# A new matmul order, load order and scheduler model, and the head outermost in the q and k casts

## The chip, the cores and the metric

The kernel runs on one core of one Trainium2 chip. The metric is the device time of one execution in microseconds (us); most executions of one kernel agree within a few tenths of a per cent. Times were taken in several sessions, in each of which the kernel before ran beside the others on the same chip. Its own median moved from 226.7 to 227.4 us between sessions, so kernels are compared by their ratio to it in the same rounds. All results were correct.

## The reference

Sliding-window attention with four sink positions (batch 4, 8 heads, 768 positions, head size 64), then a feed-forward part on its 3072 x 512 output. Cut to what matters:

```python
scores = np.matmul(q, k.transpose(0, 1, 3, 2)) / np.sqrt(64)
keep = is_sink | in_window                 # 4 sinks, window of 128
a = softmax(np.where(keep, scores, -1e9))
x = (a @ v) as 3072 x 512
h = x @ w_in                               # 512 x 2048
g = h * (1.0 / (1.0 + np.exp(-beta * h)))
return g @ w_out                           # 2048 x 512
```

## The kernel before

The program builds a list of operations, and a scheduler written in the kernel file orders it when the program is built. The order of the matmul groups on the TensorE (PE) and of the first loads is fixed by two strings that a search found. One letter is one group: T transposes q and k, C and D are scores, S sink scores, A attention output, X its transpose, h and g the two halves of a first feed-forward product for an early tile (H when whole), O four matmuls of the second product, b a small transpose of beta.

```python
PAR = {'MD': 1, 'XB': 2, 'l0': [0, 2, 6, 1, 3, 4, 9, 5, 7, 10, 8],
       'mix': 'aawwaawawawwawwaaaawwawwawwwawaa'}   # a: a q, k or v load, w: a weight load
ORDER = ('TCDTSTTDCSDSCASCTADACbXXAhhhXXThghDghgDhggThgggChhgghgShDSghSghghTghgCASCAXADOXOAhhhhXOXOgOOggOOhghg'
...                                                  # 405 groups in all
class Graph:
    LEAD, PAD, LATE = 1500, 2000, 90000
    BIAS, EARLY = 300, 100000        # a copy on the activation engine counts 300 ns more
    FILL_TO = 48000                  # fillers may stand up to here (ns of the plan)
```

The scheduler estimates when each load lands and when each engine is free; each engine is then given its own list in that order, with semaphores to wait on. Where the plan sees PE idle before 48 us, it puts in a *filler*, a matmul of ones into a free PSUM bank that nobody reads, meant to keep the clock up:

```python
    def fillers(self, t, banks, holder, new):
        while self.free["pe"] < min(t, self.FILL_TO):
            ...
            n = min(512, int((t - now) * 2.4 / slow) // 128 * 128)
            if not free or n < 128:
                return
            ...                              # append one matmul of n columns
```

Weights are loaded as f32 in 16 pieces of 512 KB and cast to bf16 before use, and so are q, k and v:

```python
    def cast_w(j):
        ...
        any_of(copies(dst, src_, {"act": 947, "dve": 602, "gp": 1060}), ...)   # the engine is chosen by the plan
    def cast(hb, n, i):
        ...
            src = stg[n][z][:, hs, :, :].rearrange("p h j d -> p j h d")       # q and k of the first half batches
            dst = x16[n][hb % NX][:, :, hs, :]
```

The first product (line 910 before, 956 after) needs such weights: four h groups need the first, third, fifth and seventh weight load in turn, four g groups the second, fourth, sixth and eighth. The activation engine then takes a tanh of it and the vector engine (DVE) multiplies; both read PSUM, and the program lets a bank be written again only after both. In the profile of before, PE's operand loads (PEld) of line 783, which reads no product, waited 1.8 us for line 917's products, in five waits.

The softmax here doesn't subtract the row's maximum and nothing guards it: scores larger than these inputs give would overflow.

## Time and profile before

| | before |
|---|---|
| time, median of the first 3 runs | 226.73 us |
| span of the profiled run | 225.4 us |
| PE busy from 20 to 200 us | 177.1 of 180 us |
| fillers | 31, of which 29 before 20 us |
| first matmul of line 910 | 19.90 us |

PE is the engine to look at: from 20 us on it is nearly always busy, so the end is set by when its stream starts, by the stream's work and by the waits within it. The prediction shows the lines of the profile on which this rests.

### The profile page before, as it was taken

Reading aid. Unit: us, or ns where it says so; the run is one execution under the profiler, and the core shown is the slowest. Engines: PE = TensorE matmul, PEld = TensorE weight load, DVE = VectorE, ACT = ScalarE, POOL = GpSimd, SP = SyncE. Lnnn points to the kernel's source line nnn. Section 1 sums busy time; section 2 is a strip of 40 time slices with the busy share of each in tenths; the row PEclk is TensorE's granted clock in tenths of the full one; section 3 lists DMA queues with packets and bytes.
Section 4 is the critical chain, followed back from the end, with each engine's and each line's share of the span. In section 5 each row is a group of like instructions: output and inputs, shape, how many; then the busy total and the mean of one; then the engine's idle time right before and its main releaser. Section 6 shows DMA issues by size and latency. Waiting matters only on the chain.

```text
span 225.4 us, 4463 instructions
## 1 busy us (share of the span) xinstructions
PE 216.1 (96%) x1699; PEld 119.9 (53%) x1720; DVE 141.0 (63%) x313; ACT 141.6 (63%) x257; POOL 66.4 (29%) x157
## 2 busy tenths in 40 slices
PE   8789999999999999999999999999999999999994
PEld 3446555555455545645564665455455556555443
DVE  1798899878757278839774478756362626455100
ACT  2495998134882857547788847777756756566221
POOL 7174345000362616352108510141435400000000
PEclk9979999999999999999999999999999999999999
DMA  7999999998999989999999999993133033101112
GB/s 159 266 320 374 360 213 311 348 250 161 219 207 224 202 198 235 189 253 221 197 239 208 185 239 220 245 256 106 47 84 81 0 84 81 49 4 47 47 47 93
DMA packets 104741, 40.95 MB, mean 182 GB/s; under 512 B 93312, under 2 KB 97680, under 8 KB 104720
## 3 DMA queue, kind: packets, MB, share of 16 engines
q1 hardware_dynamic: 103152, 40.65, 79.4%
q8 instruction: 13, 0.21, 0.4%
q10 hardware_dynamic: 1568, 0.02, 0.4%
q14 instruction: 8, 0.07, 0.1%
HBM read 27.30 MB, written 6.29 MB: 149 GB/s over the span
## 4 chain that ended last, share of the span: by engine, by line
PE 70%; DVE 10%; SPq 8%; DMA 6%; ACT 3%; issue 1%
PE P L931 31%; PE P L910 28%; SPq L635 7%; DMA v_stage<-in_v_dram 5%; DVE g L917 4%; PE P L861 4%; PE P L783 3%; DMA out_dram<-osb 2%; PE P L851 2%; SPq L891 1%; ACT t L915 1%; PE P L819 1%; PE P L1027 1%; DVE onorm L868 1%; DVE vaug L563 1%
## 5 line engine op out<-in xcount | busy, mean ns | idle before, releaser
L910 PE MATMUL P<-xT,w_in 128*128 128x384 bf16 x512 | 92.7, 327 | 0.0
L915 ACT ACTIVATE t<-P,hbeta 128x384 f32<-128x384 f32 x128 | 71.8, 586 | 32.3 <-PE P L910 24.4
L931 PE MATMUL P<-w_out,g 128*128 128x512 bf16 (+2 forms) x379 | 89.1, 371 | 1.7 <-DVE g L917 0.4
L917 DVE SCALAR_TENSOR_TENSOR g<-t,P 128x384 bf16<-128x384 f32 x128 | 67.8, 548 | 34.5 <-ACT t L915 31.8
L798 POOL TENSOR_SCALAR_AFFINE_SELECT E<-E 128x256 bf16<-128x256 bf16 (+1 forms) x109 | 52.4, 512 | 57.7 <-ACT E L792 57.7
L910 PEld LDWEIGHTS P<-xT,w_in 128*128 128x128 bf16 x512 | 48.3, 98 | 34.8 <-issue 0.8
L931 PEld LDWEIGHTS P<-w_out,g 128*128 128x128 bf16 x400 | 36.6, 98 | 37.5 <-DVE g L917 1.5
L792 ACT ACTIVATE E<-P 128x768 bf16<-128x768 f32 (+1 forms) x64 | 45.6, 760 | 14.8 <-PE P L783 14.7
L861 PE MATMUL P<-vaug,E 128*128 128x65 bf16 x352 | 19.1, 197 | 0.3 <-DVE vaug L563 0.2
L861 PEld LDWEIGHTS P<-vaug,E 128*128 128x128 bf16 x352 | 17.1, 100 | 3.6 <-ACT E L792 0.7
L558 ACT ACTIVATE osb<-P 128x512 f32<-128x512 f32 (+2 forms) x16 | 9.1, 570 | 15.2 <-PE P L931 15.1
L868 DVE TENSOR_TENSOR onorm<-P,rden 128x384 bf16<-128x384 f32 x32 | 17.4, 552 | 0.5
L783 PE MATMUL P<-qkT 64*128 64x128 bf16 (+1 forms) x256 | 16.6, 241 | 1.0 <-ACT E L792 0.4
L823 ACT ACTIVATE ES<-P 128x128 bf16<-128x128 f32 (+1 forms) x32 | 12.0, 390 | 7.0 <-PE P L819 7.0
L563 DVE CAST k<-k_stage 128x512 bf16<-128x512 f32 (+1 forms) x24 | 11.5, 477 | 6.0 <-DMA k_stage<-in_k_dram 5.7
L783 PEld LDWEIGHTS P<-qkT 64*128 64x128 bf16 x256 | 8.2, 94 | 12.4 <-issue 3.9
L851 PE MATMUL P<-vS,ES 128*128 128x130 bf16 x64 | 12.9, 223 | 0.6 <-DVE vS L686 0.4
L563 DVE CAST q<-q_stage 128x512 bf16<-128x512 f32 (+1 forms) x19 | 8.8, 465 | 7.2 <-DMA q_stage<-in_q_dram 7.1
L563 DVE CAST vaug<-v_stage 128x512 bf16<-128x512 f32 x18 | 7.9, 439 | 8.2 <-DMA v_stage<-in_v_dram 8.0
L725 POOL TENSOR_TENSOR kS<-qkT,headm 128x8 bf16<-128x8 bf16 x16 | 3.0, 209 | 32.5 <-DMA qkT<-k 28.8
L1027 PE MATMUL P<-ones 128*128 128x512 bf16 (+2 forms) x31 | 9.8, 443 | 1.2 <-POOL ones L569 1.1
L564 DVE TENSOR_SCALAR osb<-P 128x512 f32<-128x512 f32 x9 | 6.2, 690 | 6.9 <-DMA out_dram<-osb 5.2
(48 smaller groups left out, 90.5 us busy)
## 6 DMA issues: line engine op xcount, KB each, us to landing
v_stage<-in_v_dram SPq DMA_DIRECT2D x24, 256.0 KB, 4.9
out_dram<-osb SPq DMA_DIRECT2D x23, 256.0 KB, 2.5
q_stage<-in_q_dram SPq DMA_DIRECT2D x18, 256.0 KB, 4.7
k_stage<-in_k_dram SPq DMA_DIRECT2D x18, 256.0 KB, 5.6
wst<-in_moe_w_in_dram SPq DMA_DIRECT2D x5, 512.0 KB, 6.7
wst<-in_moe_w_out_dram SPq DMA_DIRECT2D x4, 512.0 KB, 8.4
g<-in_moe_w_out_dram SPq DMA_DIRECT2D x4, 512.0 KB, 8.0
q_stage<-in_q_dram SPq DMA_DIRECT2D x8, 192.0 KB, 4.7
```

Source lines behind the costliest of these rows:

```text
L563: return lambda e: e.tensor_copy(dst, at())
L635: o = add("sp", lambda e: e.dma_start(dst, src), ns, w=[("stg", n, z, j) for j in keys], dma=f"d{n}{z}{'' if i is None else i}", ring={610 ...
L783: add("pe", lambda e, dst=dst, own=own, kc=kc, rows=rows, q0=q0, nq=nq: e.matmul(dst(), tokens(own, hp, 1, rows, kc, 1)[:, 0, :], tokens(h ...
L792: add("act", lambda e, src=src, dst_=dst_: e.activation(dst_, src(), AF.Exp, bias=0.0, scale=SCALE), act_ns(256 * n), w=[(k_, z, j) for k_ ...
L798: alts = {"gp": (lambda e, d=d, sg=sg, at_=at_: e.affine_select(d, d, [[0, 2 * len(at_)], [sg, 128]], ALU.is_ge, 0.0, base=min(sg, 0), cha ...
L851: add("pe", lambda e, m=m, o0=o0: e.matmul(A()[:, o0:o0 + 2 * (D + 1)], ES[z][:, (c0 + m) * 128:(c0 + m + 1) * 128], vS[b % 2][:, 2 * hp:2 ...
L861: e.matmul(A()[:, o0:o0 + D + 1], E[z][:, i, hh, :], vaug[vz][:, kb % NK, 2 * hp + hh, :], start=a, stop=o, skip_group_check=True), 39,
L868: add("dve", lambda e: e.tensor_tensor(onorm[:, on, 2 * c0:2 * c1, :], av()[:, :, 0:D], rden[on][:, 0:2 * nb].unsqueeze(2).to_broadcast([1 ...
L910: first = add("pe", lambda e, c=c: e.matmul(hp(), w_in16[:, c, m * 128:(m + 1) * 128], xT[:, hb, c, 128 * c0:128 * c1], start=(c == 0), st ...
L915: add("act", lambda e: e.activation(tt[ti][:, 0:n], hp(), AF.Tanh, bias=0.0, scale=hbeta[:, m:m + 1]), act_ns(n) + 93, r=["hbeta"], w=[("t ...
L917: add("dve", lambda e: e.scalar_tensor_tensor(gt[hb % NG][:, m, 128 * c0:128 * c1], tt[ti][:, 0:n], 1.0, hp(), ALU.add, ALU.mult), dve_ns( ...
L931: add("pe", lambda e, m=m: e.matmul(P[:, bk[0], a:b], gt[hb % NG][:, m, t * 128:(t + 1) * 128], w_out16[:, m, a:b], start=(m == 0), stop=( ...
```

## The change

The intent: the scheduler's model was to come closer to the chip (longer and more detailed transfer times, stalls, fillers that leave room for the cost of a change between kinds of matmul; its constants are its author's estimates, not checked one by one here), the search for the matmul order and the load order was done again against several cases of it (longer transfers, a lower clock; the search itself is not shown here), and the casts of q and k for the first half batches got another order of loops. The core of the diff, with cuts:

```diff
-PAR = {..., 'l0': [0, 2, 6, 1, 3, 4, 9, 5, 7, 10, 8], 'mix': 'aawwaawawawwawwaaaawwawwawwwawaa'}
-ORDER = ('TCDTSTTDCSDSCASCTADACbXXAhhhXXThghDghgDhggThgggChhgghgShDSghSghghTghgCASCAXADOXOAhhhhXOXOgOOggOOhghg'
+PAR = {..., 'l0': [0, 1, 3, 9, 2, 10, 5, 4, 7, 6, 8], 'mix': 'aaaawawawawwwwaaaawwwwwwawwaaaa'}
+ORDER = ('TSbCTDDSCTSDTCAADTSCXXTCSAhhAXhhXgggghhhhggghghDhggDhgTghShhDgCCThgSggSDAAACXOXOAOXhOXOhhOhghOOgggOh'
 ...
-    LEAD, PAD, LATE = 1500, 2000, 90000
-    BIAS, EARLY = 300, 100000
+    LEAD, PAD, LATE = 2000, 1000, 90000
+    BIAS, EARLY = 150, 16000
-    RING, FETCH, SWITCH = 165, 900, 85
-    DEPTH = 9
+    FETCH, SHORT, SWITCH = 1150, 400, 85
+    DMA = {"nat": ((434, 580, 580, 580, 470), 64, 1200, 115, 2250, 1200), ...   # one row per kind of transfer
+    DEPTH = 5
 ...                                    # place(), stall() and fillers() follow the new model
-            src = stg[n][z][:, hs, :, :].rearrange("p h j d -> p j h d")
-            dst = x16[n][hb % NX][:, :, hs, :]
+            src = stg[n][z][:, hs, :, :]
+            dst = x16[n][hb % NX][:, :, hs, :].rearrange("p j h d -> p h j d")
```

## The prediction

> **What bounds the kernel now.** I read the page's busy shares and its row of slices first, then the busy time of each engine in five stretches, then the timeline at the places where PE stood still. The stretches:
>
> ```profile
> 0.00:20.00 20.00, 16.58 (x151) 9.29 (x152) 13.50 (x34) 11.67 (x21) 12.21 (x40) 0.91 1.01 267
> 20.00:60.00 40.00, 39.18 (x306) 21.89 (x306) 34.64 (x73) 25.96 (x48) 9.22 (x20) 1.00 1.02 275
> 60.00:120.00 60.00, 58.53 (x503) 32.16 (x508) 41.35 (x97) 40.97 (x77) 23.03 (x51) 1.00 1.11 217
> 120.00:200.00 80.00, 79.37 (x618) 44.65 (x627) 44.88 (x99) 53.06 (x96) 21.92 (x48) 1.00 0.62 128
> 200.00:225.40 25.40, 22.40 (x129) 11.96 (x129) 6.64 (x12) 9.94 (x18) 0.00 (x0) 1.00 0.14 53
> ```
>
> After the length stand PE, weight loads, DVE, ACT and POOL, then granted clock, DMA share, GB/s. PE is the bound: from 20 us to 200 us it is idle for 0.82 + 1.47 + 0.63 = 2.92 us. The first 20 us are different: 3.4 us idle, and of the 16.58 us busy most is filler that computes nothing (the same stretches for line 1027):
>
> ```profile
> 0.00:20.00 20.00, 8.95 (x29) 0.91 1.01 267
> 20.00:60.00 40.00, 0.83 (x3) 1.00 1.02 275
> ```
>
> In that start the clock also fell once (windows of 1 us, same columns as the first table):
>
> ```profile
> 13.00:14.00 1.00, 0.51 (x10) 0.23 (x6) 0.95 (x4) 1.00 (x3) 1.00 (x3) 1.00 1.08 300
> 14.00:15.00 1.00, 0.98 (x14) 0.63 (x14) 1.00 (x4) 0.82 (x3) 1.00 (x3) 0.76 0.94 333
> 15.00:16.00 1.00, 1.00 (x16) 1.00 (x14) 1.00 (x5) 1.00 (x2) 0.29 (x2) 0.50 1.03 374
> 16.00:17.00 1.00, 1.00 (x9) 0.41 (x7) 1.00 (x2) 0.99 (x3) 0.81 (x1) 0.50 1.03 338
> 17.00:18.00 1.00, 1.00 (x17) 0.83 (x14) 0.89 (x5) 0.30 (x2) 0.80 (x2) 0.53 1.05 366
> ```
>
> PE was half idle just before (0.54 and 0.51 us in the two windows from 12 to 14), and then ran some 3.4 us at 0.50. The first matmul of the feed-forward part (line 910) starts at 19.90 us. From then on PE is nearly full, so the time of the end is about the start of that stream, plus its work, plus its waits.
>
> What limits the stream up to 60 us is the arrival of data: the DMA share is 1.02 and DVE is busy 34.64 of 40 us. The timeline shows two places. The eighth weight load, the last one of line 910's weights, lands at 29.54 us by the trace's semaphores, DVE casts it only at 30.55, and the matmul that needs it follows 0.1 us after the cast:
>
> ```profile
> 30.55 0.69 DVE L563 CAST w_in<-wst 128x1024 bf16<-128x1024 f32 x1
> ...
> 31.34 0.33 PE L910 MATMUL P<-xT,w_in 128*128 128x384 bf16 x1
> ```
>
> The second weight matrix does the same to line 931's first matmuls: the load lands at 37.17, the cast runs from 37.71 for 0.78 us, and PE, which had put in a filler, starts at 38.43.
>
> The later waits are short. Four matmuls of line 931 take 0.86 us from start to start when nothing is missing. At 72.15 they take 1.33 until the next start, which waited for a DMA transpose:
>
> ```profile
> 72.15 1.03 PE L931 MATMUL P<-w_out,g 128*128 128x512 bf16 x4
> 73.48 0.51 PE L783 MATMUL P<-qkT 64*128 64x256 bf16 x8 [0.31 <-DMA qkT<-k]
> ```
>
> So a busy sum hides part of a wait (0.31 is shown of 0.47 lost). I went through all starts of PE after 60 us in this way: 0.47 at 72, 0.57 at 82, 0.60 at 84, and some ten of 0.1 to 0.3. Without the unavoidable cost of changing kinds of matmul, which I put at 0.09 a change, they add to about 4 us. The same sum from 20 to 60 us is about 3 us, most of it between 34 and 38.5 us.
>
> [...] casts of 512 elements with outermost 8 (v) have a median of 430 ns, and casts of only 384 elements with outermost 3 (q and k of the first half batches) take 411 to 425 where nothing disturbs them. [...] a v load (256 KB in runs of 256 bytes) lands 1.15 us after the one before, a q or k load of the first half batches (192 KB in 768-byte runs) 0.55 to 0.65.
>
> **The change part by part.** Nearly all lines of the diff change constants of the scheduler that runs when the program is built. On the chip only the result differs: which group of matmuls comes when, where fillers stand, which engine casts or masks, and the order of loads. Counting the letters of both order strings gives the same multiset (405 groups: 96 H, 32 h, 32 g, 100 O and so on), so the matmuls are the same; runs of 64-row groups (C, D) go from 37 to 36. The work on PE is therefore equal but for fillers. The output switch and the accumulation flag on fillers change nothing at run time.
>
> *Casts.* [...] Doubling 512 elements to 1024 adds 685 - 430 = 255 ns [...]: about 0.36 us in place of 0.42. 13 of the 16 casts are on DVE now: 13 x 0.064 = 0.83 us of DVE, all before 32 us. Two or three of them lie on the way to the first transposes.
>
> *First loads.* Before: q0 q1 q3 k0 k1 q2 v1 k2 k3 v2 v0. After: q0 k0 k1 v1 q1 v2 k2 q2 k3 q3 v0. The first k lands as load 2 in place of 4, and by the landings of before (3.68, 4.75, 5.80, 6.46) at about 4.75 in place of 6.46. So the first transpose of k, at 6.96 now, can come near 5.3. But v0 stays last of 11, lands near 12.48 as now, and the first attention output (13.30) needs it. Of the 1.7 us nothing is left there by itself; but more groups of C, D, S, T are done by then. From there I put the order's groups end to end with their measured lengths (T 0.34, half-batch A 0.36 or 0.53, h or g 0.33): about 3 us of work and latency to the first h in place of 6.6. So the first L910 could be at 17 us. It needs a weight load, though, which now comes after four loads of q and k in place of two: landed about 16.8, cast by 17.5 to 17.9. Gain 2 us there.
>
> *How much of the 2 us survives.* The eighth weight load has the 11 first loads, 7 q or k loads of the second half batch and 7 other weights before it in both orders. It lands where it does now, near 29.5. The group that needs it (13th g) stands after 16.9 us of PE work in the new order, 16.5 in the old. At the earliest it starts at 29.5 + 0.7 = 30.2 against 31.34, which with the 0.4 of work more makes at most 1.6 us. The next gate is the first line 931: same loads before it, same work before it (21.8 us): 37.2 + 0.7 = 37.9 against 38.43, 0.5 us. The third gate is the transposed k of the third half batch, landed at 58.32 now; all loads up to it are the same bytes, so it stays; the first group using it now starts at 59.40 after 43.0 us of work, and would start at 58.4 or later after 43.7: at most 1.7 us. I take 1.0 us of gain carried past 60 us.
>
> *Later waits.* About 4 us are to be had from 60 us on. The new search has DMA times nearer those of the trace and puts attention groups later (12th to 15th C after 62 to 68 us of work in place of 56 to 69), so I let it save 0.9 of the 4. The tail, 222.5 to 225.4 us, has the same last groups and stays.
>
> Sum: 226.7 - 1.0 - 0.9 = 224.8.
>
> **The rivals.** (1) *The start is the bound*: 14 us pass beyond the 5.9 us of work before the first h; if the 2 us, and the half clock's 1.7 (half of 3.4), all reached the end, it would be near 222.5. For it: PE is full after 20 us. Against: the three gates above, with equal bytes before each. (2) *DMA is the bound up to 60 us*: the gates do not move and the earlier start turns into fillers and waits before them; only later waits change, 225.5 to 227. For it: DMA share 1.02; against: DVE adds about 1 us at the first gate (29.54 to 30.55), which the shorter casts can relieve. (3) *The search fitted its model, not the chip*: new waits on DMA or PSUM banks of the same sort appear elsewhere; 227 to 229. For it: the old order came from such a search and has 4 us of late waits.
>
> **Range and chances.** The gates allow 0.5 to 1.7 us and the late waits anything from +1 to -2.5 us, so 222.6 to 227.0 should hold it 8 times in 10. Faster by 2% needs 222.2: nearly all of both terms, 0.08. Slower by 2% needs 4.5 us more waits: 0.03. Within 2%: 0.89.
>
> **What would show it.** Right: 128x384 casts on DVE near 0.36; first line 910 at 17 to 18.5 us; 13th g near 30.2 to 31; fillers under 8.95 us before 20 us; first line 931 within 1 us of 38; PE's last start 1 to 3 us earlier; equal tail. Wrong: a first line 931 or a 60 us mark that comes over 2 us earlier (then rival 1, and the loads were not the gate), or losses after 60 us well off 3 us.

The sum came to 226.7 - 1.0 - 0.9 = 224.8 us. The 64 ns of a cast stand as an estimate from the trace of before: casts of 384 elements took 411 to 425 ns, nearly the 430 of 512 elements, although 512 elements more cost 255 ns (685 - 430); at that rate 128 elements less are a quarter of it, 64 ns.

What the traces say of three more figures: a start of line 783 came 0.258 us after the last one of line 910 and 0.312 us after the last one of line 931, where a line's own next start came after 0.163 and 0.216 us (medians from 20 us on, before), so the 0.09 us of a change of kind is measured. The clock stood at 0.50 from 14.52 to 17.93 us, 3.41 us. Fillers of 512 columns at full clock took 0.38 us each before and after, so the flag on them shows no effect.

## The result, and the profile after

| | before | after |
|---|---|---|
| median, same rounds, 6 runs each | 226.91 us (226.55 to 227.74) | 226.56 us (226.15 to 226.88) |
| ratio | | 0.9981, 95% interval 0.996 to 1.0001 |
| span of the profiled run | 225.4 us | 224.6 us |

The verdict is "same". A forecast gain of 1.9 us became one of 0.35 us. In a later session the changed kernel ran again (226.48 us, ratio 0.9966, interval 0.9934 to 0.9999), so a gain is likely, but small: 0.2 to 0.35%.

The five stretches of the kernel after (start and end, length, then busy time of PE, weight loads, DVE, activation engine and POOL with instruction counts, granted clock, DMA share, GB/s), to be held against those of before in the prediction:

```profile
0.00:20.00 20.00, 18.70 (x175) 9.86 (x176) 12.65 (x33) 13.40 (x24) 10.34 (x37) 1.00 1.02 273
20.00:60.00 40.00, 39.86 (x305) 21.84 (x304) 30.79 (x65) 28.69 (x54) 11.03 (x21) 1.00 0.99 273
60.00:120.00 60.00, 59.68 (x516) 32.59 (x514) 40.95 (x94) 43.08 (x83) 22.35 (x48) 1.00 1.07 210
120.00:200.00 80.00, 80.00 (x627) 44.28 (x626) 45.31 (x98) 54.38 (x100) 22.71 (x48) 1.00 0.68 133
200.00:225.40 25.40, 21.72 (x128) 11.62 (x125) 6.64 (x12) 10.03 (x18) 0.00 (x0) 1.00 0.14 52
```

PE is busier in every stretch up to 200 us, and from 20 to 60 us DVE has 3.85 us less to do and the activation engine 2.73 us more. But a busy PE is not a working PE, as the same view of the filler line (1075) shows:

```profile
0.00:20.00 20.00, 11.14 (x40) 3.90 (x40) 1.00 1.02 273
20.00:60.00 40.00, 3.49 (x13) 1.11 (x13) 1.00 0.99 273
```

There were 0.83 us of fillers from 20 to 60 us before, and there are 3.49 us now. Without them PE worked 38.35 us of those 40 before and 36.37 us after. So the place where time went is in that stretch.

**A measure that fillers cannot hide: the lag.** For each group of matmuls I took from the trace its start, and subtracted the undisturbed length (start to start, where nothing was missing) of all groups before it. The difference is the time that has been lost so far. If it grows, PE waited, whether a filler covered the wait or not. The absolute losses depend on which length is called undisturbed (by up to 2 us from 60 to 200 us, when the traces are worked through with other choices); the differences between kernels move by some 0.2 us only. The lag, in us, at the first group after each time:

| kernel | 20 us | 30 us | 40 us | 60 us | 200 us | lost 20 to 60 | lost 60 to 200 |
|---|---|---|---|---|---|---|---|
| before | 14.02 | 14.78 | 16.36 | 16.47 | 20.24 | 2.45 | 3.77 |
| after | 12.77 | 14.87 | 16.62 | 16.79 | 19.55 | 4.02 | 2.76 |
| after, second profile | 13.27 | 15.42 | 17.16 | 17.37 | 19.73 | 4.10 | 2.36 |

The new start is 1.25 us ahead at 20 us (0.75 in the second profile; that start differs by up to 0.7 us from profile to profile, so I compare what is lost within one profile). Ten microseconds later nothing of it is left. From 60 us on the new kernel loses 1.0 to 1.4 us less, and that is what remains.

Where the head start goes is best seen in the timeline of PE. Before (start, length, engine, line, operation), the groups of line 910 follow one another without a hole from 19.90 us:

```profile
19.90 1.14 PE L910 MATMUL P<-xT,w_in 128*128 128x384 bf16 x6
20.87 0.50 PE L880 MATMUL P<-ident,onorm 128*128 128x128 bf16 x6
```

After, the same stretch is pieced together with fillers (line 1075):

```profile
20.04 0.81 PE L956 MATMUL P<-xT,w_in 128*128 128x384 bf16 x4
20.69 0.33 PE L1075 MATMUL P<-ones 128*128 128x384 bf16 x1
...
21.06 0.81 PE L1075 MATMUL P<-ones 128*128 128x512 bf16 x3
21.71 2.76 PE L956 MATMUL P<-xT,w_in 128*128 128x384 bf16 x16
24.31 0.38 PE L1075 MATMUL P<-ones 128*128 128x512 bf16 x1
24.53 1.15 PE L956 MATMUL P<-xT,w_in 128*128 128x384 bf16 x6
25.52 0.97 PE L1075 MATMUL P<-ones 128*128 128x512 bf16 x4
26.33 1.14 PE L956 MATMUL P<-xT,w_in 128*128 128x384 bf16 x6
```

The lag grew by 0.35 us in these 7 us before and by 1.96 us after. In the trace of after this loss has three places.

- Some 0.85 us up to the first g at 21.71 us. This g needs the second weight load and the transposed attention output. DVE casts that load only from 20.74 to 21.53 us (it had landed at 18.14), and the transposes (X) start at 20.88 us, after which the activation engine copies their result from 21.26 to 21.75 us. In the order of before, T and h groups stand between the X and the g (20.87 to 21.87 us) and nothing is lost.
- 0.22 us before the fifth g at 24.53 us, which waits for the cast of the fourth weight load (DVE, 23.79 to 24.48 us). The load had landed at 22.51 us.
- 0.81 us before the ninth h at 26.33 us, which waits for the cast of the fifth weight load (DVE, 25.32 to 26.01 us) and then for fillers. The load had landed at 24.45 us.

These two casts in DVE's timeline of after:

```profile
23.79 0.69 DVE L609 CAST w_in<-g 128x1024 bf16<-128x1024 f32 x1
...
25.32 0.69 DVE L609 CAST w_in<-g 128x1024 bf16<-128x1024 f32 x1
```

(Both loads are staged in a tile named g.) By the trace's semaphores the first three weight loads land at 15.71, 17.12 and 19.58 us before, and at 16.23, 18.14 and 21.13 us after, because the new load order puts four q and k loads ahead of the first (two before) and six ahead of the third (four before). But no wait stands before the h groups that need the third load (from 23.01 us), and the fourth and fifth loads land 0.3 us sooner than before (22.84 and 24.77 there). The three losses are waits for a copy and for casts that stand late in DVE's list.

The eighth weight load lands at 28.55 us now, a microsecond sooner than before, but its cast (DVE, line 609) runs only at 31.56 us and the 13th g follows it:

```profile
31.56 0.69 DVE L609 CAST w_in<-wst 128x1024 bf16<-128x1024 f32 x1
...
32.30 0.50 PE L956 MATMUL P<-xT,w_in 128*128 128x384 bf16 x2
```

The late waits are fewer. Where a transposed k came late at 72 us before, the timeline of after shows no wait; its nearest idle time of PE is one for the transposed attention output:

```profile
74.62 1.64 PE L956 MATMUL P<-xT,w_in 128*128 128x384 bf16 x9 [0.26 <-DMA xT<-onorm]
```

### The profile page after: what moved, and what is told of

The parts are those of the page before. It is cut to its first block, busy times and chain, and to the rows that moved or that the text cites. A ratio compares the mean times of both kernels' runs of the same rounds, so it can differ in the third digit from the quotient of the medians.

```text
span 224.6 us, 4534 instructions
## 1 busy us (share of the span) xinstructions
PE 220.0 (98%) x1742; PEld 120.2 (54%) x1742; DVE 136.3 (61%) x301; ACT 149.6 (67%) x274; POOL 66.4 (30%) x152
## 4 chain that ended last, share of the span: by engine, by line
PE 87%; ACT 5%; DVE 5%; DMA 2%; issue 0%; POOL 0%; POOLq 0%
PE P L956 35%; PE P L977 34%; PE P L829 5%; PE P L1075 5%; PE P L907 3%; ACT E L838 2%; DMA xT<-onorm 2%; PE P L865 2%; DVE g L963 2%; PE P L897 1%; DVE onorm L914 1%; ACT qkT L604 1%; PE P L743 1%; ACT t L961 1%; DVE E L855 1%; PE P L926 1%
## 5 line engine op out<-in xcount | busy, mean ns | idle before, releaser
L956 PE MATMUL P<-xT,w_in 128*128 128x384 bf16 x512 | 94.8, 326 | 0.3 <-DMA xT<-onorm 0.3
L977 PE MATMUL P<-w_out,g 128*128 128x512 bf16 (+2 forms) x400 | 93.2, 371 | 0.0
L844 POOL TENSOR_SCALAR_AFFINE_SELECT E<-E 128x256 bf16<-128x256 bf16 (+1 forms) x109 | 56.1, 545 | 74.8 <-ACT E L838 74.4
L604 ACT ACTIVATE osb<-P 128x512 f32<-128x512 f32 (+2 forms) x23 | 13.3, 580 | 26.3 <-PE P L977 26.3
L609 DVE CAST q<-q_stage 128x512 bf16<-128x512 f32 (+1 forms) x22 | 11.0, 499 | 8.0 <-DMA q_stage<-in_q_dram 8.0
L1075 PE MATMUL P<-ones 128*128 128x512 bf16 (+3 forms) x53 | 14.6, 397 | 1.1 <-POOL ones L615 1.1
L912 DVE RECIPROCAL rden<-P 128x6 f32<-128x6 f32 x32 | 6.1, 190 | 10.6 <-PE P L907 10.3
L609 DVE CAST vaug<-v_stage 128x512 bf16<-128x512 f32 x21 | 10.4, 499 | 3.3 <-DMA v_stage<-in_v_dram 3.3
L855 DVE TENSOR_TENSOR E<-E,maskS 128x512 bf16<-128x512 bf16 x16 | 8.0, 505 | 6.4 <-ACT E L838 6.2
L609 DVE CAST k<-k_stage 128x512 bf16<-128x512 f32 (+1 forms) x20 | 8.2, 424 | 0.9 <-DMA k_stage<-in_k_dram 0.8
```

The lines of the kernel that those rows point to most:

```text
L604: return lambda e: e.activation(dst, at(), AF.Copy, bias=0.0, scale=scale)
L609: return lambda e: e.tensor_copy(dst, at())
L844: alts = {"gp": (lambda e, d=d, sg=sg, at_=at_: e.affine_select(d, d, [[0, 2 * len(at_)], [sg, 128]], ALU.is_ge, 0.0, base=min(sg, 0), cha ...
L956: first = add("pe", lambda e, c=c: e.matmul(hp(), w_in16[:, c, m * 128:(m + 1) * 128], xT[:, hb, c, 128 * c0:128 * c1], start=(c == 0), st ...
L977: add("pe", lambda e, m=m: e.matmul(P[:, bk[0], a:b], gt[hb % NG][:, m, t * 128:(t + 1) * 128], w_out16[:, m, a:b], start=(m == 0), stop=( ...
L1075: G.filler = lambda j, n: lambda e: e.matmul(P[:, j, 0:n].rearrange("p (a b) -> p a b", b=128), ones[:, :], ones[:, :].unsqueeze(1).to_bro ...
```

## The experiments

### The casts alone, and each half of the rest

**e1_casts** is the kernel before with the two cast lines of the change. Nothing else differs; the scheduler's plan is identical.

> The kernel before with one part of the change alone: the head outermost in the q and k casts of the first half batches. The scheduler's durations are the same, so every engine runs the same instructions in the same order. If the casts matter (my prediction's first term): DVE casts of 384 elements fall from 415-425 ns to about 350 to 370 where nothing disturbs them, 13 of them, and the time falls by 0.1 to 0.5 us (ratio 0.998 to 0.9995). Rival (the plan of the engines paces the start): the casts get shorter and the time stays, ratio 1.000 within 0.001.

Measured: 226.87 us, ratio 0.9997 (0.9969 to 1.0025). The casts fell from 411 to 425 ns to 348 to 361 ns where nothing disturbs them, and in the changed kernel nine of the 13 on DVE took 320 to 360 ns. In the timelines, first a cast of before, then one of after:

```profile
28.18 0.42 DVE L563 CAST q<-q_stage 128x384 bf16<-128x384 f32 x1
```

```profile
13.60 0.36 DVE L609 CAST q<-q_stage 128x384 bf16<-128x384 f32 x1
```

So this part does what it should to DVE, and the time does not move.

**e2_new_order_old_plan** is the kernel before with the new PAR and ORDER, **e3_old_order_new_plan** the kernel after with the old ones.

```diff
-PAR, ORDER of its own kernel
+PAR, ORDER of the other kernel
```

> The kernel before with the new order of groups and loads, but the old constants of the scheduler (old DMA times, old mask times, old filler rule, old casts). Theory A (order and constants belong together; the fewer late waits come from the order): waits after 60 us as few as in the kernel after, a worse start, time 226 to 229. Rival (the new order by itself is the gain): time at or under the kernel after, 226.5 or less. The scheduler's own plan for it ends at 230.9 against 224.5 for before, which would be ratio 1.02 if the chip followed the plan.

> The kernel after with the old order of groups and loads. Theory A: the late waits of the kernel before come back (about 3.8 us lost from 60 to 200 us in place of 2.8) and the start gets fillers of the new plan; time 227 to 230. Rival (the constants are the gain, through engine choice and fillers): late waits stay few, 226 to 226.6. The plan ends at 230.5.

Measured: 235.30 us (ratio 1.0363) and 232.91 us (1.025). Both are far slower, mostly after 60 us: e2 loses 11.2 us there and e3 6.7 us, where the kernel before loses 3.8. The waits of PE from 60 to 200 us show it (what waited, for what, total, times, longest); first e2, then e3:

```profile
PE P L910 <- DMA xT<-onorm: 2.8, 2, 2.0
```

```profile
PE P L829 <- DMA qkT<-k: 1.9, 1, 1.9
```

An order and the model it was searched with belong together; neither is the good half of the change.

### The fillers

**e4_no_fill_20** is the changed kernel without the 13 fillers that its plan places from 20 us on; every other instruction keeps its place.

```diff
-        self.ops = new
+        self.ops = new = [o for o in new if o.eng != "pe" or o.group is not None or not 20000 <= o.at < 99999]
```

> The kernel after without the fillers planned from 20 us on (11 rows of them on PE), all else instruction for instruction the same. Rival B (fillers planned for data that had already landed hold PE up from 20 to 37 us): PE's work at 40 us is 1 to 3 us ahead of the kernel after, time 0.5 to 2 us less. Theory A (DVE's order, made for later landings, holds the casts and PE waits for them with or without fillers): the fillers turn into idle time, time less by 0 to 0.5 us.

Measured: 225.55 us (225.32 to 226.13), ratio 0.9932 (0.991 to 0.9954). In a later session it ran again beside the unchanged kernel after, as **e10_no_fill_again** and **e9_after_again**.

> The changed kernel as it is, as a control on the same chip and in the same rounds: 226.4 to 226.9, ratio 0.997 to 1.0.

> The changed kernel without its fillers from 20 us on, a repeat beside the control. If the late fillers really cost about 1 us: 0.7 to 1.3 us under the control. If the first result was luck of its session: within 0.4 us of the control.

Measured: 226.48 us for the kernel after and 225.50 us without the late fillers. They cost 0.98 us. The timeline of e4 shows how at one place:

```profile
21.42 4.04 PE L956 MATMUL P<-xT,w_in 128*128 128x384 bf16 x22 [0.36 <-DVE w_in L609]
25.85 1.15 PE L956 MATMUL P<-xT,w_in 128*128 128x384 bf16 x6 [0.38 <-DVE w_in L609]
```

Before 25.85 us PE waits 0.38 us for the cast of the fifth weight load, which ends at 25.79, and goes on 0.06 us later. In the kernel after the same cast ends at 26.01 (25.32 and 0.69 us in DVE's timeline), but PE is inside four fillers from 25.52 us and goes on at 26.33, 0.32 us after it. The plan had placed the fillers by its own estimate of that cast, and the h group stands behind them in PE's list. From 20 to 40 us the lag grows by 3.51 us in e10 and by 3.85 and 3.89 us in the two profiles with late fillers (3.34 in e4, whose first group after 20 us comes just after a loss of 0.19 us). That is about 0.4 us of the 0.98. The rest stands at other places in the two pairs of profiles (after 60 us in one, before 20 us in the other), and I could not place it.

**e5_no_fill_8_20** takes away the fillers between 8 and 20 us instead, with the same edit and other bounds.

> The kernel after without the fillers planned from 8 to 20 us (those later and earlier stay). If those fillers keep the clock up and that matters: the clock falls to 0.5 once between 12 and 25 us and the time rises by 1 us or more. If fillers only hold PE up (as the ones after 20 us turned out to do): the time falls by 0.2 to 0.6 us against the kernel after (ratio to before 0.995 to 0.997) with or without a fall of the clock. If the start is gated by data: time within 0.2 us of the kernel after, although the clock falls.

Measured: 227.44 us median (225.64 to 227.94). The mean granted clock over the span was between 0.985 and 0.992 in five of six runs. Those took 226.72 to 227.94 us, and the one run at 1.0 took 225.64 us. The windows of 1 us from its profile (same columns as the stretches) show the fall:

```profile
13.00:14.00 1.00, 0.52 (x5) 0.24 (x5) 0.92 (x5) 0.19 (x1) 0.38 (x1) 0.71 1.11 333
14.00:15.00 1.00, 1.00 (x12) 0.69 (x10) 0.75 (x3) 0.79 (x3) 0.19 (x1) 0.50 1.05 375
```

So in the new order the early fillers hold the clock: with them it was 0.998 or more in all 12 runs of the kernel after. A fall goes with some 1.9 us (the median of the runs with it, 227.51, less the single run without), but that is one run, and the time does not follow the depth: the two runs at 0.985 took 227.38 and 227.53 us, the three at 0.991 and 0.992 took 226.72 to 227.94. In the one run without a fall no early filler was missed. Whether the early fillers pay as a whole is not shown: e5 stands at a ratio of 1.0000 (0.9966 to 1.0033), the kernel after in other sessions at 0.9966 to 0.9981, within that interval. In the kernel before the same fall costs nothing that can be seen: in one session its runs at a clock of 0.992 had spans of 225.0 to 225.9 us and those without a fall 225.1 to 226.4 us.

### Which engine paces the stretch from 20 to 40 us

Without its late fillers the kernel still loses about as much between 20 and 40 us. My first theory was that DVE casts the weights too late (three microseconds after landing for the eighth, 0.8 to 1.3 us for the fourth and fifth). **e6_casts_at_landing** is e4 with seven weight casts moved forward in DVE's list to where their load lands:

```diff
+        earlier(self, [(39, 37), (42, 41), (45, 43), (48, 46), (53, 49), (61, 57), (64, 59)])   # places in DVE's list
```

> As e4 (no fillers from 20 us), and seven weight casts on DVE moved one to four places forward in DVE's order, to where the trace of the kernel after shows that their loads have landed; all other engines and DVE's other work instruction for instruction the same. Theory A (DVE's order, planned for later landings, is what PE waits for): the eighth w_in cast starts near 29.2 in place of 31 us, the 13th g near 30 to 30.5 in place of 31.8, PE's state at 60 us 0.5 to 1.5 us ahead of e4, time 0.4 to 1.2 us below e4 (225.5), so about 224.3 to 225.1. Rival (PE is held by the tanh and product chain or by later loads, w_out and v, not by the place of the casts): the casts start earlier, the 60 us state and the time stay within 0.3 us of e4.

Measured: 226.95 us, ratio 0.9988, 1.4 us slower than e4. The eighth load was cast 2.3 us sooner (28.80 in place of 31.09 us), but the 13th g started at 31.71 us in place of 31.83, and the lag at 40 us rose from 16.13 to 16.94. The elementwise products, after which the PSUM banks can be written again, had to stand back for the casts: PE has new waits for them of 0.29 us at 28.5 and 0.28 us at 33.7 us. Of these 0.81 us, 0.6 us is a later start, there already at 20 us.

At first sight the theory falls. From 27 us on it does: these casts, moved, only make other work late. Between 21 and 27 us the trace says the opposite. In e6 the fourth and fifth casts end at 23.19 and 25.35 us, and the groups that wait for them in e4 (see its two lines above) follow without a hole:

```profile
22.05 4.78 PE L956 MATMUL P<-xT,w_in 128*128 128x384 bf16 x28 [0.36 <-DVE w_in L609]
26.76 0.34 PE L829 MATMUL P<-qkT 64*128 64x256 bf16 x4
```

From the third h to the end of the fourteen h and g groups that begin with the first g, the lag grows by 0.79 us in e6, against 1.59 us in e4, in e10 and in e8 (reckoned alike for all; e8, which comes below, has these casts in their old places and starts as late as e6). So the place of these two casts in DVE's list did hold PE there, with the loads where they were.

The second theory was that the activation engine paces PE, because it has no gap from 27.3 to 38.6 us. **e7_less_on_act** takes two pieces of its work away (e4 with a transposed-k copy moved to DVE and a k cast to POOL), **e8_more_on_act** puts one on it (e4 with the eighth weight cast moved there from DVE).

```diff
+        transfer(self, [('act', 42, 'gp', 38), ('act', 46, 'dve', 57)])    # e7: engine and place, to engine, before place
+        transfer(self, [('dve', 53, 'act', 43)])                           # e8
```

> The kernel without fillers from 20 us on (225.55 us), with two pieces of work taken off the activation engine between 31 and 34.4 us, where it has no gap: the last transposed-k copy of that half batch (0.81 us) goes to the vector engine, ahead of its two v casts, where it is idle for 1.3 us before 35.9 us, and the cast of one k piece (0.56 us) goes to the idle POOL. Theory C (the activation engine empties PSUM and paces the TensorE there): the exponentials of 31.6 to 35.8 us come 0.5 to 1.3 us earlier, the group deficit at 40 us falls from 16.1 to 15.5 or less, and the time is 0.4 to 1 us less: 224.5 to 225.2. Rival (the vector engine's chain through the elementwise product or the data paces it): deficit at 40 us within 0.3 us of 16.1 and time within 0.3 us, or worse where the copy stands in the vector engine's way.

> The reverse: the kernel without fillers from 20 us on, with the cast of the eighth weight load (0.69 us on the vector engine at 31.09 us) moved to the activation engine [...] before its exponential of 31.6 us. Theory C: [...] the deficit at 40 us rises from 16.1 to 16.6 to 17.0, and the time is 0.4 to 1 us more (226 to 226.6). Rival (vector engine paces): its chain comes 0.69 us earlier and the deficit falls by up to 0.7, time 224.9 to 225.5.

Measured: e7 226.15 us (ratio 0.9959), with 1.76 us lost from 30 to 40 us, as in e4 and e10 (1.73 and 1.72), and a profile only 0.24 us behind e10's at 200 us, so that most of the 0.65 us between their medians has no place that I could find; e8 226.76 us (0.997), lag at 40 us 17.69, of which 0.8 us over e4 was there at 20 us. (Casts of 128x1024 on the activation engine took 1.08 us in the kernel before and 1.05 us in the kernel after.) The numbers of e8 fit the theory, but its waits from 28 to 40 us give another reason:

```profile
PEld P L956 <- ACT w_in L604: 1.2, 1, 1.2
```

PE waited for that very cast, which now stood in another queue. And relieving the engine, in this form, gained nothing, so nothing speaks for this theory.

The third theory was DVE as a whole: it has hardly a gap from 20 to 32.5 us. **e11_casts_on_pool** is e4 with three weight casts put on POOL, which is idle from 21 to 28.3 us. They are those of the second, sixth and seventh loads; the expectation calls the second the third.

```diff
+        transfer(self, [('dve', 35, 'gp', 32), ('dve', 45, 'gp', None), ('dve', 48, 'gp', None)])
```

> The kernel without fillers from 20 us on (225.5 us), with three of the weight casts (the third, sixth and seventh loads, 0.69 to 0.78 us each on the vector engine at 20.7, 26.8 and 28.2 us) put on POOL, which is idle from 21 to 28.3 us. Theory D (the vector engine, which has no gap from 20 to 32.5 us, paces the TensorE there as a whole, so that a mere change of its order as in the casts-at-landing run could not help): the later casts and elementwise products come 0.7 to 1.5 us earlier, the group deficit at 40 us falls from 16.2 to 15.2 to 15.8, time 224.5 to 225.1. Rival (landings and the length of the chain through both engines pace it, no single engine): deficit at 40 us within 0.3 us of 16.2, time within 0.4 us of 225.5; worse if POOL's cast takes longer than 1.2 us and a group waits for it.

Measured: 225.51 us, ratio 0.9948, lag 14.51 at 30 us and 16.22 at 40 us, the same as e10. DVE was busy 16.10 us from 20 to 40 us in place of 17.67, and once it waited for a load, the third:

```profile
21.35 0.79 DVE L609 CAST w_in<-wst 128x1024 bf16<-128x1024 f32 x1 [0.59 <-DMA wst<-in_moe_w_in_dram]
```

So DVE's load as a whole does not pace PE here. But the two casts that PE waits for, of the fourth and fifth loads, stayed on DVE and ended at 24.36 and 25.89 us (24.40 and 25.93 in e10). And the cast of the second load, now done at 20.65 us on POOL, left the first loss as it was: there the transposed attention output alone is enough.

### The landing and the casts of the weights

**e12_weights_sooner** is e11 with the third, fourth and fifth weight loads issued ahead of the two q and k loads that stood between them, the casts of those two pieces later on the activation engine, and two weight casts earlier on DVE:

```diff
+        transfer(self, [('sp', 19, 'sp', 24), ('sp', 22, 'sp', 24),          # a k load and a q load after the fifth weight load
+                        ('act', 24, 'act', 32), ('act', 30, 'act', 33),      # their casts later
+                        ('dve', 39, 'dve', 37), ('dve', 42, 'dve', 40),      # casts of the fourth and fifth weight loads earlier
+                        ...])                                                # and the three moves of e11
```

> The casts-on-POOL kernel (225.5 us, deficit 12.9 at 20 us, 14.5 at 30, 16.2 at 40) with the third, fourth and fifth weight loads issued ahead of the two q and k loads that went between them, those two pieces cast later on the activation engine, and the casts of the fourth and fifth loads ahead of two elementwise products each on the vector engine. Theory E (between 20 and 28 us the first expert groups wait for the weights, which the saturated transfers land no sooner than in the kernel before, so the gain of the new start is lost there): the third to fifth loads land 0.6 to 1.5 us sooner, the deficit at 30 us falls from 14.5 to 13.3 to 13.9. If it then stays, 224.6 to 225.0 us; if later waits take it back, the deficit at 40 us is over 15.9 and the time over 225.2. Rival (the chain TensorE, activation, vector engine back to TensorE through the PSUM banks paces the first expert groups): deficit at 30 us within 0.3 us of 14.5, time within 0.4 us of 225.5.

Measured: 225.46 us, ratio 0.9943 (0.992 to 0.9966). (The DMA share, called saturated in the expectation, was 1.05 in e11 from 20 to 25 us.) The third to fifth loads landed at 20.46, 21.82 and 23.23 us (21.49, 22.86 and 24.77 in e10). The run of fourteen h and g groups lost 0.67 us from 20.95 us on (0.94 in e10, after 0.53 just before it, and 1.46 in e11), so that the lag after it was 13.52 us in place of 14.40. The edit moved two things, the loads and the casts of the fourth and fifth of them. The casts alone are enough for this gain: e6, with no load moved, lost no more over the same groups (0.79 us from the third h on, and 0.80 in e12). That the earlier landing adds anything is not shown. But the gain was gone by 28.5 us (lag 14.35), and the timeline of the activation engine says why:

```profile
25.15 0.51 ACT L604 ACTIVATE k<-k_stage 128x384 bf16<-128x384 f32 x1
...
26.03 0.52 ACT L604 ACTIVATE q<-q_stage 128x384 bf16<-128x384 f32 x1
...
27.37 0.83 ACT L838 ACTIVATE E<-P 128x768 bf16<-128x768 f32 x1
```

The two casts that I had moved stood in front of the tanh and the exponential (line 838) for which the next scores waited 0.55 us. Whether the gain would be kept without this side effect was open, so two more kernels were run. **e13_casts_off_act** is e12 with those two casts on POOL, **e14_eighth_sooner** the same with the eighth weight cast also ahead of a copy and a product on DVE.

```diff
+                        ('act', 24, 'gp', None), ('act', 30, 'gp', None)     # e13
+                        ('dve', 53, 'dve', 51)                               # e14 only
```

> The weights-sooner kernel (deficit 12.85 at 21 us, 13.5 at 26.2, but 14.35 again at 28.5, 225.46 us) with the two q and k casts that it had put on the activation engine at 25.2 and 26.0 us (0.5 us each) moved to POOL, which waits there for a weight load. If those two casts are what took the gain back (the group at 27.7 us waited 0.55 us for an exponential of the activation engine): deficit at 28.5 us 13.5 to 13.9. If the gain is then kept to the end: 224.6 to 225.1 us. If the next gate (the eighth weight load, landed at 28.5 and cast at 31.05) takes it: deficit at 32 us again 14.7 or more, and 225.3 to 225.6 us.

> The same with the cast of the eighth weight load put ahead of the transposed-q copy and one elementwise product on the vector engine, so at about 29.5 instead of 31.05 us. If the eighth load's cast is the next gate: deficit at 32 us 14.0 to 14.5 instead of 14.9, and 224.5 to 225.0 us. If what the copy feeds waits instead: no gain on the one without it, within 0.3 us.

Measured: e13 **224.96 us** (224.66 to 225.34), ratio 0.9903 (0.9877 to 0.9929); e14 224.87 us (its five fast runs, 224.69 to 225.75), ratio 0.9906 (0.9872 to 0.994). In e13 the fourteen groups run with one hole at the start and none inside:

```profile
22.06 4.56 PE L956 MATMUL P<-xT,w_in 128*128 128x384 bf16 x27 [0.42 <-ACT xT L604]
26.56 0.34 PE L829 MATMUL P<-qkT 64*128 64x256 bf16 x4
```

| kernel | lag at 20 us | 30 us | 40 us | 60 us | 200 us | lost 20 to 30 |
|---|---|---|---|---|---|---|
| e10, no late fillers | 12.75 | 14.54 | 16.26 | 16.46 | 18.78 | 1.79 |
| e11, casts on POOL | 12.89 | 14.51 | 16.22 | 16.39 | 18.71 | 1.62 |
| e12, weights sooner | 12.84 | 14.49 | 16.10 | 16.23 | 18.68 | 1.65 |
| e13, and no casts in the way | 13.02 | 14.04 | 15.75 | 15.89 | 18.23 | 1.02 |
| e14, and the eighth cast sooner | 13.44 | 14.50 | 16.29 | 16.41 | 18.71 | 1.06 |

(In e11 and e12 the first group after 20 us comes just after a loss of 0.19 us, so that their loss is shown that much too small beside the others.) The loss from 20 to 30 us fell to 1.02 us and 1.06 us, in two kernels, and what was saved there is still saved at 200 us. Bringing the eighth cast forward gains nothing: e14 has a start 0.4 us worse, and from there runs like e13. What is left of the loss is the first one, the wait for the transposed attention output (0.42 us in the line above); no run took it away. e13 is the fastest kernel, 1.0% under the kernel before and some 0.7% under the kernel after (0.9903 against 0.9981 and 0.9966, from different sessions). In e6 the casts came early but the products stood back for them; in e13 POOL takes three weight casts and two others (POOL busy 14.56 us from 20 to 60 us, 11.69 in e10), and DVE has a little less to do (30.32 us, 31.19 in e10), the activation engine about as much (28.76, 28.97). How much of the gain is due to each of the moves was not taken apart.

## Why the prediction was right or wrong

The forecast was 224.8 us from 226.7; the kernel took 226.56 us beside 226.91. It lies in the range, but most of the gain did not come.

**Right: the casts.** The estimate of 64 ns less for each holds: 411 to 425 ns became 348 to 361 ns (e1). Why the order of loops matters is not shown. That they would be worth little by themselves is shown by e1.

**Right: the later waits.** The prediction let the new order save 0.9 us after 60 us; the loss there fell from 3.77 to 2.76 us, by 1.0 us (by 1.4 in the second profile). e1, which has the plan of before, loses 0.4 us less than before there, so the saving may be as small as 0.6 us, and the 0.9 was a guess that came out well. That e2 and e3 are slow just there shows that neither the order nor the model alone brings it.

**Right in kind, too large: the start.** The first line 956 was to come at 17 to 18.5 us and came at 18.82; the lag at 20 us was 1.25 us less, not 2 us less. Fillers before 20 us were to be under 8.95 us and were 11.14 us. The tail is equal (2.89 us from PE's last end to the end of the span, 2.88 before).

**Wrong: the step "I take 1.0 us of gain carried past 60 us".** Measured is a loss of 0.3 us at 60 us (0.9 in the second profile) in place of a gain of 1.0 us. The step rested on three gates, of which the first was the eighth weight load, with the argument that equal bytes stand before it in both orders. That is true of the eighth (it even landed 1 us sooner), but the 13th g, which needs it, came at 32.30 us and not at 30.2 to 31, for the start gain was gone long before. The first gate is not at 29.5 us but at 21 to 26 us, and it is not a landing. The prediction looked for no gate between the first weight load and the eighth. But the new order puts four g groups right behind the transposes whose copied result they need (0.85 us lost, read from the traces; no run took it away), and the casts of the fourth and fifth loads stand 1.3 and 0.9 us behind their landings in DVE's list (0.22 and 0.81 us lost, of which 0.3 us is fillers). That the place of these casts holds PE is shown by e6, where no load was moved and both holes are gone; e12 to e14, which moved the loads too, lose as little there. The gain lasts to the end only where the moved casts do not get in the way of products, tanh or exponentials (e13 and e14, not e6 and e12). About 0.5 us of the time came back so (e13 against e10, from different sessions). The second gate was misread as well: the first line 931 at 38.43 us starts before the cast from 37.71 us ends (38.49), for its first two matmuls need the load before.

**Not foreseen: fillers that cost.** The prediction treated fillers as harmless, as something that an earlier start "turns into". 13 of them stand from 20 us on, at one place shown beyond the end of the wait that they fill, and taking them away is worth 0.98 us (e9 and e10). With both causes removed the kernel runs at 224.96 us, which is near where the forecast put the change (224.8), but by luck: it named neither.

**The rivals.** The second, transfers as the bound up to 60 us with 225.5 to 227 us, came nearest: the head start did turn into fillers and waits. But the waits found up to 33 us were not for the transfers: the loads that the waiting groups needed had landed. The first (the whole start gain and the half clock reach the end) is refuted by the lag at 30 us; the half clock of before cost nothing that could be seen. The third, new waits that the model doesn't see, is true between 20 and 30 us only.

**Open:** no run tells whether the load order of e12 to e14 does anything beside their moved casts. Open are also whether another order of X and g would win back the first 0.85 us, where about half of the 0.98 us of the late fillers arises, why the start varies by 0.7 us, and what holds PE from 30 to 40 us. There all kernels of the new order that have no late fillers lose 1.6 us or more and none of the moves on one engine changed that for the better; the kernel before loses as much (1.58 us).

## What to carry to other kernels

When an order is changed, check every consumer between the first and the last load, and for each of them when its load lands, when its cast ends and when its other input is ready. Equal bytes before the last load say nothing of those in between, and a load that has landed is of no use while its cast stands behind other work. When a move fails as a whole, as e6 did, look at the place that it was made for before giving up the theory. A filler stands in PE's list like any other instruction (after a cast PE went on 0.32 us later behind four of them, 0.06 us later in e4 without), so it should stand only where the clock falls without it, as it did in five of six runs of e5. Compare the useful work done by a time, not the busy share; and when a wait is taken away, look at what the move itself put into another engine's list (e12) before concluding that the gain is absorbed.

## Further figures from the traces

- The fall of the clock: in the kernel before PE was busy 0.54 and 0.51 us in the two windows of 1 us before it, and from 12 us to the fall at 14.52 us no idle stretch of PE was longer than 0.40 us. In e5 PE was busy 0.52 us in the window in which it came (13 to 14 us, clock 0.71). In e1, which has the same lists as the kernel before, no run had a mean clock under 0.998. Which busy share is enough is not shown.
- Casts from f32 to bf16: 128x1024 took 1.05 us on POOL in e11 (written as an affine select) against 0.69 us on DVE, and 128x384 took 0.50 us on POOL in e7, 0.50 and 1.02 us in e13, against 0.56 us on the activation engine in e4.
